# Drains on GpSimd, later row sums and fills, and no clearing of stored tiles in a fused FFT, expert and softplus kernel

## The chip, the cores and the metric

The kernel runs on one core of a Trainium2 chip. The time is that of one execution on the device, in microseconds (us), of the core that takes longest; here there is one. The engines are named as in the profile: PE (TensorE matmuls) and PEld (its weight loads), DVE (VectorE), ACT (ScalarE), POOL (GpSimd) and SP (SyncE, which here only issues DMAs). A q behind the name (POOLq) is the engine's sequencer: instructions that move no tensor data, such as waits, branches and drains.

## What is computed

Three stages follow each other. A real FFT filter over each of 8 batches of 3072 tokens with 256 channels; a top-1 mixture of 8 experts with room for `capacity` = 768 tokens each; and a softplus layer over all 24576 tokens.

```python
Y = np.fft.rfft(x, axis=1) * F;  y = np.fft.irfft(Y, n=S, axis=1)       # per batch
e = argmax(y @ w_gate);  slots 0..767 of each expert are filled in order of the tokens
y2 = gate_w * (relu(tok @ w1[e]) @ w2[e])          # tokens without a slot: zeros
h = y2 @ w_in;  g = np.maximum(h, 0.0) + np.log1p(np.exp(-np.abs(h)))
out = g @ w_out
```

For a token without a slot y2 is zero, so g is ln 2 everywhere and its row of the output is ln 2 times the sums of w_out's columns. All such rows are equal.

## The kernel before

The experts fill up early, so the kernel runs the filter and the gating for the first three batches only (STATIC = 3) and keeps a branch for the other case, which is not entered here (`tc.If` on `flag`, read by every engine at the end, L1266 and L1267).

The 8 × 768 slots are 16 units of 384 slots (class `Unit`). A unit gathers its tokens (`load_x`, three indirect DMAs of 128 rows issued by POOL, tile xd, L704), transposes them, multiplies by w1 and w2 (py, yh, yl), then runs 16 blocks of the softplus layer: `wi` makes pi in PSUM (L791), ACT takes abs, exp and ln (L649 to L652), DVE adds up g (L657), ACT rounds it to gh (L803), POOL makes the rest gl = g - gh (L808), and `wo` adds gh·woh, gh·wol and gl·woh into po (L823). At a unit's end `take` copies po to three tiles ot on DVE (L830), and `store` scatters them with three indirect DMAs that POOL issues (L835). POOL also splits the experts' weights (w1l and w2l, L689).

The order is written out by hand from step 16 on. A step t is one block of one unit, t = 16 v + i. `ev(t, order, ...)` files a call under its step, and `step(t)` runs a step's calls by their order W2, WI, SP, WO, SUM, W1, TAKE, TR, AHEAD. Block t has its `wi` and softplus in step t, its gh and gl in step t + 2 (`sp_split`), its `wo` in step t + 4. Each engine runs its instructions in the order in which they were written, so what stands first on an engine holds up what stands behind it. Three tiles g go around, so g of one block waits for gl of the block three before. There are seven tiles ot.

Class `Rest` makes the rows of tokens without a slot. `sums(k, c)` is one reduction on DVE over 32 columns of woh or wol (tile cs, L851), 16 of them; `zero` makes ln 2 (zt); `rows` multiplies (pz, L863) and copies the result to cs; `fill(a)` is one DMA of 512 KB from SP that writes that row over 512 tokens of the output (L869). The first 18 fills cover the three batches that have slots, and the stores of the units wait for them, since they write over the fills. The other 30 fills go out later at every third step and are declared free of the stores.

After the last step three memsets on POOL clear the first column of the last unit's tiles ot (L1259). A memset may start when the store that reads the tile has landed. Then come the flag's load (L1266), the branch (L1267) and the end of the program (L1407).

Of the kernel before, what the change touches and what calls it, by code (L numbers as in the profile page):

```python
# [17 lines left out]
NB, S, D, E = 8, 3072, 256, 8  # L18
# [8 lines left out]
STATIC = 3  # L27
# [174 lines left out]
def body(tc, cap, x, ff, fx, wg, w1, w2, win, wout, m1, m2, m3, m4, small, out):  # L202
    nc = tc.nc
# [671 lines left out]
    with tc.manual_schedule():  # L875
# [17 lines left out]
        units = [Unit(e, h) for h in range(nunit) for e in range(E)]  # L893
# [201 lines left out]
        W2, WI, SP, WO, SUM, W1, TAKE, TR, AHEAD = range(9)  # L1095
# [21 lines left out]
        for v in range(HEAD):  # L1117
            u = units[v]
# [53 lines left out]
        for v, u in enumerate(units):  # L1172
            for i in range(KI):
                t = 16 * v + i
# [33 lines left out]
        def ev(t, order, fn, *args):  # L1208
            if t < STEPS:
                return  # L1210
            at.setdefault(t, []).append((order, len(at.get(t, ())), fn, args))

        def step(t):
            for *_, fn, args in sorted(at.pop(t, ()), key=lambda e: e[:2]):
                fn(*args)
# [12 lines left out]
        rest = Rest()  # L1228
        for v, i in to_split:
            ev(split_at(v, i), AHEAD, split_w)  # L1230
        for v, u in enumerate(units):
            b = 16 * (v - 2)
            if v >= HEAD:
                ev(b - 16, AHEAD, load_x, u)
                for k in range(2):
                    ev(b - 7 + 2 * k, TR, u.tr_x, k)
            for j in range(8 if v > 1 else 0):
                ev(b + 2 * j - 3, W1, u.w1, j)
                ev(b + 2 * j, W2, u.w2, j)
            for i in range(KI):  # L1240
                t = 16 * v + i
                ev(t, WI, u.wi, i)
                ev(t + 2, SP - 0.5, u.sp_split, i)
                ev(t, SP, u.sp_act, i)
                ev(t, SUM, u.sp_sum, i)
                ev(t + 4, WO, u.wo, i)
            ev(16 * v + 19, TAKE, u.take)
            for t in range(3):
                ev(max(16 * v + 21, 40 + 3 * v) + t * (v < len(units) - 1), AHEAD, u.store, "out", [t])
        for t in range(16):  # L1250
            ev(16 + t // 2, SUM, rest.sums, t // 8, t % 8)
        ev(24, SUM, rest.zero)
        ev(26, TR, rest.rows)
        for a in range(NT // 512):
            ev(28 + a // 2 if a < STATIC * S // 512 else 3 * a, AHEAD, rest.fill, a)
        for t in range(min(at), max(at) + 1):
            step(t)
        for ot in units[-1].ot:
            nc.gpsimd.memset(ot[:, 0:1], 0.0)  # L1259
        stm.close()  # L1260
        stw.close()
        P.close.close()
# [4 lines left out]
    with tc.If(fv > 0):  # L1267
# [53 lines left out]
        with ExitStack() as st:  # L1321
# [9 lines left out]
            with tc.For_i(0, E, 1) as e:  # L1331
                with tc.For_i(0, nunit, 1) as h:
                    u = Unit(e, h)
# [77 lines left out]
```

## Time and profile before

| | |
|---|---|
| median of 3 runs | 1059.43 us (1055.43 to 1059.56) |
| the profiled execution | 1056.44 us |
| its span, first to last instruction | 1054.7 us |
| PE busy | 1024.0 us, 97% |
| ACT, POOL, DVE busy | 778.3, 598.9, 467.9 us |

The span says how long the program ran between its first and last instruction on the chip; the execution's own time has 1.7 us around it. A share of busy time is a mean over stages: the filter stage runs to about 205 us, the written-out steps from 290 us to about 1035 us, and the end of the program after that. Step t can be found in the trace by its six matmuls `pi` of L791: those of step 20 begin at 303.00 us, those of step 48 at 397.61 us, those of step 64 at 449.14 us.

### The profile page before, as it was taken

To read this page: it belongs to the slowest core of one execution; us is meant where nothing else is said; L and a number is where in the kernel's file an instruction comes from. 1 tells how busy PE (TensorE), PEld (TensorE's weight loads), DVE (VectorE), ACT (ScalarE), POOL (GpSimd) and SP (SyncE) were. 2 spreads that over 40 slices of the span, in tenths; PEclk is the share of its full clock that TensorE was granted. 3 is DMA by queue.
4 is the path that set the end of the run, shared out by engine and by line. 5 is a ranking of instruction groups with operands and counts; after the bars stand their busy time and mean duration, and the time that the engine had idled before them with its cause. 6 is when DMAs were issued, how large, how long until landed. Compare 5 with 4: busy or idle time off the path is not lost.

```text
span 1054.7 us, 19035 instructions
## 1 busy us (share of the span) xinstructions
PE 1024.0 (97%) x7112; PEld 952.2 (90%) x7112; DVE 467.9 (44%) x895; ACT 778.3 (74%) x1612; POOL 598.9 (57%) x563
## 2 busy tenths in 40 slices
PE   8999999999999999999999999999999999999992
PEld 7655676699999999999999999999999999999992
DVE  3855898888874332333232333233333333323220
ACT  4465478778867787777787878787877787878981
POOL 0512544688654676565757575757575756564552
PEclk9999999999999999999999999999999999999996
DMA  9977728654114822333323232322121211000000
GB/s 279 292 233 233 230 86 269 196 176 150 55 46 156 298 71 80 110 104 115 127 99 133 85 130 100 111 80 72 43 77 46 66 51 61 21 16 6 11 17 18
DMA packets 72823, 120.04 MB, mean 114 GB/s; under 512 B 6928, under 2 KB 46736, under 8 KB 72720
## 3 DMA queue, kind: packets, MB, share of 16 engines
q1 hardware_dynamic: 65424, 96.69, 28.9%
q0 software_dynamic: 4608, 12.59, 3.4%
q10 hardware_dynamic: 2688, 9.44, 2.7%
q8 instruction: 58, 0.95, 0.4%
q14 instruction: 45, 0.37, 0.1%
HBM read 71.51 MB, written 47.19 MB: 113 GB/s over the span
## 4 chain that ended last, share of the span: by engine, by line
PE 87%; DMA 4%; issue 2%; POOL 2%; DVE 2%; ACT 1%; SPq 0%; POOLq 0%; ACTq 0%; DVEq 0%
PE pi L791 24%; PE po L823 24%; PE pw L737 13%; PE py L766 12%; PE p L437 3%; PE p L385 2%; PE p L332 2%; PE p L398 2%; DMA xt<-in_x_dram 2%; DMA fr<-in_ff_dram 2%; PE p L357 1%; POOL gl L808 1%; PE pt L714 1%; PE p L536 1%; DMA fi<-in_fx_dram 1%
## 5 line engine op out<-in xcount | busy, mean ns | idle before, releaser
L657 DVE SCALAR_TENSOR_TENSOR g<-pi,ln 128x384 f32<-128x384 f32 x256 | 142.6, 557 | 490.2 <-ACT ln L652 450.0
L808 POOL TENSOR_TENSOR gl<-g,gh 128x384 fp32r<-128x384 f32 x256 | 260.8, 1022 | 112.2 <-ACT gh L803 106.1
L823 PE MATMUL po<-woh,gh 128*128 128x256 f32 x768 | 216.4, 282 | 3.9 <-DVE ot L830 3.9
L823 PE MATMUL po<-woh,gl 128*128 128x256 f32 x768 | 216.2, 281 | 0.0
L823 PE MATMUL po<-wol,gh 128*128 128x256 f32 x768 | 216.0, 281 | 0.0
L649 ACT ACTIVATE ab<-pi 128x384 f32<-128x384 f32 x256 | 124.7, 487 | 121.7 <-PE pi L791 98.3
L791 PE MATMUL pi<-yh,wih 128*128 128x384 f32 x512 | 172.8, 338 | 1.0 <-DVE g L657 1.0
L791 PE MATMUL pi<-yh,wil 128*128 128x384 f32 x512 | 173.1, 338 | 0.0
L791 PE MATMUL pi<-yl,wih 128*128 128x384 f32 x512 | 172.9, 338 | 0.0
L823 PEld LDWEIGHTS po<-woh,gh 128*128 128x128 f32 x768 | 144.0, 187 | 6.4 <-ACT ab L649 2.5
L823 PEld LDWEIGHTS po<-wol,gh 128*128 128x128 f32 x768 | 145.0, 189 | 0.0
L823 PEld LDWEIGHTS po<-woh,gl 128*128 128x128 f32 x768 | 144.7, 188 | 0.0
L652 ACT ACTIVATE ln<-ab 128x384 f32<-128x384 f32 (+1 forms) x257 | 134.8, 525 | 8.2
L650 ACT ACTIVATE ab<-ab 128x384 f32<-128x384 f32 (+1 forms) x257 | 134.7, 524 | 8.2
L689 POOL TENSOR_TENSOR w1l<-ws,w1h 128x512 fp32r<-128x512 f32 x64 | 83.2, 1301 | 100.1 <-ACT w1h L684 71.0
L803 ACT CAST gh<-g 128x384 fp32r<-128x384 f32 x256 | 130.2, 509 | 0.7 <-DVE g L657 0.5
L689 POOL TENSOR_TENSOR w2l<-ws,w2h 128x512 fp32r<-128x512 f32 x64 | 83.1, 1300 | 75.1 <-ACT w2h L684 73.9
L791 PEld LDWEIGHTS pi<-yh,wih 128*128 128x128 f32 x512 | 96.2, 188 | 1.3 <-DVE g L657 1.3
L791 PEld LDWEIGHTS pi<-yl,wih 128*128 128x128 f32 x512 | 96.2, 188 | 0.0
L791 PEld LDWEIGHTS pi<-yh,wil 128*128 128x128 f32 x512 | 96.2, 188 | 0.0
L377 POOL TENSOR_TENSOR z<-z,t 128x512 f32<-128x512 f32 x36 | 45.9, 1276 | 76.0 <-DVE t L372 60.9
L766 PE MATMUL py<-hh,w2h 128*128 128x384 f32 x256 | 88.2, 344 | 0.0
(141 smaller groups left out, 1897.4 us busy)
## 6 DMA issues: line engine op xcount, KB each, us to landing
ws<-in_w_dram SPq DMA_DIRECT2D x128, 256.0 KB
out_dram<-cs SPq DMA_DIRECT2D x48, 512.0 KB
xt<-in_x_dram SPq DMA_DIRECT2D x24, 384.0 KB
mid<-s ACTq DMA_DIRECT2D x16, 384.0 KB
rowsd<-yt SPq DMA_DIRECT2D x16, 384.0 KB
it<-mid SPq DMA_DIRECT2D x24, 256.0 KB
wst<-in_win_dram SPq DMA_DIRECT2D x8, 512.0 KB
wst<-in_wout_dram SPq DMA_DIRECT2D x8, 512.0 KB
```

The lines of the kernel that those rows point to most:

```text
L377: nc.gpsimd.tensor_tensor(out=z, in0=z, in1=t2, op=ALU.add)
L649: nc.scalar.activation(out=ab[:, :n], in_=h, func=ACTF.Abs)
L650: nc.scalar.activation(out=ab[:, :n], in_=ab[:, :n], func=ACTF.Exp, scale=-1.0)
L652: nc.scalar.activation(out=ln[:, :n], in_=ab[:, :n], func=ACTF.Ln, bias=1.0)
L657: nc.vector.scalar_tensor_tensor(out=g[:, :n], in0=h, scalar=0.0, in1=ln[:, :n], op0=ALU.max, op1=ALU.add)
L689: nc.gpsimd.tensor_tensor(out=lo, in0=self.ws.pop(i), in1=hi.bitcast(F32), op=ALU.subtract)
L737: nc.tensor.matmul(ps, lhsT=a[:, k, fs], rhs=b[:, k], start=(n == 0), stop=(n == 5))
L766: nc.tensor.matmul(self.py[d], lhsT=a[:, j % 2, ds], rhs=b, start=(j == 0 and n == 0), stop=(j == 7 and n == 2))
L791: nc.tensor.matmul(pi, lhsT=a[i // 2][:, i % 2, k], rhs=b[:, k], start=(n == 0), stop=(n == 5))
L803: nc.scalar.copy(gh, self.g[i])
L808: nc.gpsimd.tensor_tensor(out=gl, in0=g, in1=gh.bitcast(F32), op=ALU.subtract)
L823: nc.tensor.matmul(self.po[t], lhsT=a[:, ts], rhs=b[:, i], skip_group_check=True, start=(i == 0 and n == 0 and t != 1), stop=(i == KI - 1 ...
```

## The change

Four things change in the written-out steps.

- A `drain` on POOL is put at the end of step 16 v + 13 of each unit. Calls for steps below 16 are dropped, so there are 15 drains, in steps 29, 45, ..., 253. The program gives them no wait and no tensor.
- The 16 row sums stand one in a step in steps 16 to 31 (two in a step in steps 16 to 23 before), and at the step's end (AHEAD) where they stood behind g (SUM).
- The rows are made in step 33 (26 before), the 18 fills begin in step 35 (28 before), and the stores of the first two units begin in steps 46 and 49 (40 and 43 before). From the third unit on the stores stay where they were.
- The three memsets on the last unit's tiles ot are gone.

```diff
-                ev(max(16 * v + 21, 40 + 3 * v) + t * (v < len(units) - 1), AHEAD, u.store, "out", [t])
+                ev(max(16 * v + 21, 46 + 3 * v) + t * (v < len(units) - 1), AHEAD, u.store, "out", [t])
+            ev(16 * v + 13, AHEAD, nc.gpsimd.drain)
         for t in range(16):
-            ev(16 + t // 2, SUM, rest.sums, t // 8, t % 8)
+            ev(16 + t, AHEAD, rest.sums, t // 8, t % 8)
         ev(24, SUM, rest.zero)
-        ev(26, TR, rest.rows)
+        ev(33, TR, rest.rows)
         for a in range(NT // 512):
-            ev(28 + a // 2 if a < STATIC * S // 512 else 3 * a, AHEAD, rest.fill, a)
+            ev(35 + a // 2 if a < STATIC * S // 512 else 3 * a, AHEAD, rest.fill, a)
         for t in range(min(at), max(at) + 1):
             step(t)
-        for ot in units[-1].ot:
-            nc.gpsimd.memset(ot[:, 0:1], 0.0)
```

DVE's row at the end of the first unit, steps 18 to 20, before. A row is a line, an operation, out<-in and the size; cs is a row sum, hl a part of the expert layer, ot the copies that free po.

```order
L657 SCALAR_TENSOR_TENSOR g<-pi,ln 128x384
L851 TENSOR_REDUCE cs<-woh 128x32 x2
L657 SCALAR_TENSOR_TENSOR g<-pi,ln 128x384
L851 TENSOR_REDUCE cs<-woh 128x32 x2
L749 SCALAR_TENSOR_TENSOR hl<-pw,hh 128x384
L830 COPY ot<-po 128x256 x3
L657 SCALAR_TENSOR_TENSOR g<-pi,ln 128x384
```

The same place after the change.

```order
L657 SCALAR_TENSOR_TENSOR g<-pi,ln 128x384
L851 TENSOR_REDUCE cs<-woh 128x32
L657 SCALAR_TENSOR_TENSOR g<-pi,ln 128x384
L749 SCALAR_TENSOR_TENSOR hl<-pw,hh 128x384
L830 COPY ot<-po 128x256 x3
L851 TENSOR_REDUCE cs<-woh 128x32
L657 SCALAR_TENSOR_TENSOR g<-pi,ln 128x384
```

The two sums that stood ahead of hl and of the copies ot in step 19 are one sum behind them.

POOL's row in steps 48 to 51, before. w1l and w2l are weight splits, the DMA of xd is the gather for a later unit.

```order
L689 TENSOR_TENSOR w1l<-ws,w1h 128x512
L704 DMA xd<-rowsd,gi_2361 128x256 x3
L808 TENSOR_TENSOR gl<-g,gh 128x384 x2
L689 TENSOR_TENSOR w2l<-ws,w2h 128x512
L808 TENSOR_TENSOR gl<-g,gh 128x384 x2
```

The same place after the change, from the split in step 48 to gl in step 51 (the stores of steps 46 and 47 stand further up).

```order
L689 TENSOR_TENSOR w1l<-ws,w1h 128x512
L835 DMA out_dram<-ot,si_2362 24576x256
L704 DMA xd<-rowsd,gi_2361 128x256 x3
L808 TENSOR_TENSOR gl<-g,gh 128x384
L835 DMA out_dram<-ot,si_2362 24576x256
L808 TENSOR_TENSOR gl<-g,gh 128x384
L689 TENSOR_TENSOR w2l<-ws,w2h 128x512
L835 DMA out_dram<-ot,si_2362 24576x256
L808 TENSOR_TENSOR gl<-g,gh 128x384
```

The stores of the first two units, which stood in steps 40 to 45 with no gather near, now stand around the gather of step 48. The drains are not in these listings, which leave out instructions without tensors; a drain of step 16 v + 13 stands on POOL behind gl of that step and ahead of gl of the next.

## Rows read from the trace of the kernel before

**Rows 1.** The page, engines: busy us, share of the span, instructions.

```profile
PE 1024.0 (97%) x7112; PEld 952.2 (90%) x7112; DVE 467.9 (44%) x895; ACT 778.3 (74%) x1612; POOL 598.9 (57%) x563
```

**Rows 2.** Busy time by stretch: us; PE, PEld, DVE, ACT, POOL; clock; DMA share, GB/s.

```profile
290.00:340.00 50.00, 47.04 (x309) 46.26 (x309) 29.12 (x45) 36.08 (x78) 25.70 (x24) 1.00 0.26 84
340.00:957.00 617.00, 617.00 (x4096) 614.63 (x4095) 194.86 (x370) 478.98 (x1004) 386.02 (x357) 1.00 0.27 92
1035.00:1054.70 19.70, 0.78 (x7) 0.57 (x5) 1.09 (x3) 0.00 (x0) 3.27 (x6) 0.59 0.07 24
```

**Rows 3.** Timeline of PE, step 20: start, us, instruction [idle before <- releaser].

```profile
303.87 0.34 PE L791 MATMUL pi<-yh,wil 128*128 128x384 f32 x1
306.19 0.36 PE L823 MATMUL po<-woh,gh 128*128 128x256 f32 x1 [1.99 <-DVE ot L830]
```

**Rows 4.** Timeline of DVE, step 19.

```profile
302.93 1.99 DVE L851 TENSOR_REDUCE cs<-woh 128x32 f32<-128x512 f32 x2
304.84 0.55 DVE L749 SCALAR_TENSOR_TENSOR hl<-pw,hh 128x384 fp32r<-128x384 f32 x1
305.30 1.07 DVE L830 COPY ot<-po 128x256 f32<-128x256 f32 x3
```

**Rows 5.** Timeline of POOL, steps 48 to 50.

```profile
401.04 1.30 POOL L689 TENSOR_TENSOR w1l<-ws,w1h 128x512 fp32r<-128x512 f32 x1 [2.29 <-ACT w1h L684]
402.49 1.04 POOL L704 DMA_INDIRECT xd<-rowsd,gi  x1
...
406.17 2.01 POOL L808 TENSOR_TENSOR gl<-g,gh 128x384 fp32r<-128x384 f32 x2
```

**Rows 6.** Timeline of POOL, step 45: a store behind gl.

```profile
392.02 1.00 POOL L835 DMA_INDIRECT out_dram<-ot,si  x1 [0.17 <-issue]
```

**Rows 7.** Timeline of PE, step 51: the first matmul that reads gl.

```profile
407.37 0.29 PE L823 MATMUL po<-woh,gl 128*128 128x256 f32 x1
```

**Rows 8.** Busy time by stretch, around the end of the first fills.

```profile
360.00:363.00 3.00, 3.00 (x24) 3.00 (x24) 0.56 (x1) 2.90 (x7) 0.80 (x1) 1.00 1.02 380
366.00:370.00 4.00, 4.00 (x31) 4.00 (x30) 0.56 (x1) 3.46 (x8) 1.71 (x3) 1.00 0.00 0
```

**Rows 9.** Timeline of POOL, the last store and the memsets.

```profile
1038.75 0.98 POOL L835 DMA_INDIRECT out_dram<-ot,si  x1 [0.30 <-issue]
...
1041.93 0.10 POOL L1259 MEMSET ot<- 128x1 f32 x1 [1.93 <-DMA out_dram<-ot,si]
```

**Rows 10.** Lines L1266, L1267: engine, operation, count: ns min/median/max, first and last start.

```profile
L1266 POOLq TENSOR_LOAD <-flag x1: 502/502/502, 1041.9 to 1041.9; - x1
L1267 POOLq INC_SWDGE_SEM  x1: 2112/2112/2112, 1043.3 to 1043.3; - x1
```

**Rows 11.** Drains at the end (L1407) and the start (L1401) of the program.

```profile
L1407 POOLq DRAIN  x3: 40/107/8049, 1045.8 to 1054.4; - x3
L1407 ACTq DRAIN  x2: 8/8/8, 1036.0 to 1054.1; - x2
...
L1401 POOLq DRAIN  x1: 181/181/181, 0.3 to 0.3; - x1
```

**Rows 12.** The page, DMA issues: POOL's indirect DMAs.

```profile
xd<-rowsd,gi POOLq DMA_INDIRECT x48
out_dram<-ot,si POOLq DMA_INDIRECT x48
```

**Rows 13.** Timeline of POOL, steps 61 to 64, around the place of the third drain.

```profile
443.96 1.02 POOL L808 TENSOR_TENSOR gl<-g,gh 128x384 fp32r<-128x384 f32 x1 [1.80 <-ACT gh L803]
446.23 1.30 POOL L689 TENSOR_TENSOR w2l<-ws,w2h 128x512 fp32r<-128x512 f32 x1 [1.25 <-ACT w2h L684]
...
449.27 1.01 POOL L808 TENSOR_TENSOR gl<-g,gh 128x384 fp32r<-128x384 f32 x1 [0.76 <-ACT gh L803]
452.58 1.30 POOL L689 TENSOR_TENSOR w1l<-ws,w1h 128x512 fp32r<-128x512 f32 x1 [2.29 <-ACT w1h L684]
```

**Rows 14.** Timeline of PE, step 64: the first matmul that reads gl of step 62.

```profile
450.42 0.28 PE L823 MATMUL po<-woh,gl 128*128 128x256 f32 x1
```

## The prediction

> **What bounds the kernel now.** I read the page's line of engines first: PE is busy 97% of the span [rows 1]. That leaves the question where the other 3% lie, so I cut the written-out steps into stretches [rows 2]. From 340 to 957 us PE is busy all of 617.00 us: in these steps nothing can be won, and an edit there can only cost. Two stretches have room. From 290 to 340 us PE lacks 2.96 us. From 1035 us on it has 0.78 us of work in 19.70 us: PE, ACT and DVE are done, and POOL runs alone to the end. The largest piece of that end is one row: of the three drains on POOL in the program's last lines one takes 8.049 us, starting at 1045.8 us [rows 11]. It ends at 1053.8 us, 0.9 us before the span does. So the change has to be judged at four places: the stall at 304 us, the memsets, the long drain, and whatever the added instructions delay in steps where PE has no slack.
>
> **The row sums.** In step 20 the last matmul of `wi` starts at 303.87 us and the next one, the first of `wo`, at 306.19 us, with 1.99 us of idle time that the copies ot ended [rows 3]. DVE shows why: two sums of 1.99 us in all, then hl, then ot from 305.30 us [rows 4]. In the new order the sums of that step stand behind ot. Without the 1.99 us ahead of them hl and ot would start about 1.9 us earlier, limited by when hl's input is there, and later units, which have no sums at all, show no such stall: PE is full there [rows 2]. I take 2.0 us as won; the bounds are 1.0 us (if the single sum of step 18 still pushes) and 2.0 us. The sums that move to steps 24 to 31 lie on DVE, which is busy 194.86 of 617 us from 340 us on [rows 2]; at one sum of about 1.0 us [rows 4] in a step of about 3.2 us they fit behind g. I cost them at nothing; if one delayed a copy ot or a g, it would be by at most its own 1.0 us, once or twice. Rows and fills are the same instructions in later steps and PE pays for them as before.
>
> **The stores that meet the gather.** This is a cost. Before, in step 48, POOL has w1l at 401.04 us, the three gathers from 402.49 us, and gl of step 49 at 406.17 us [rows 5]; as two gl take 2.01 us it ends at 407.18 us. PE reads that gl at 407.37 us without a wait [rows 7]: 0.2 us to spare. Now the stores of steps 46 to 51 stand there, and the one of step 48 is ahead of the gathers. A store costs 1.00 us and 0.17 us of issue behind gl, or 0.30 us behind another indirect DMA [rows 6, 9]. So gl of step 49 comes 1.3 us later, at 408.5 us, and PE waits 1.1 to 1.2 us at step 51. Behind it POOL has a store, gl of step 50, a split, a store and gl of step 51: 1.1 + 1.0 + 1.3 + 1.1 + 1.0 us, which ends at 414.0 us. The reader of that last gl stands two steps of 3.2 us behind the one of 407.37 us, and PE is 1.2 us late: 415.0 us, in time. I take +1.2 us, bounds 0 and +2. The fills are over before these stores: the DMA engines are full to 363 us and at zero from 366 us [rows 8], so the 18 fills end near 365 us for a first store in step 40; both move by seven and six steps, and the margin of some 11 us shrinks by one step of 3.2 us. Nothing waits there.
>
> **The memsets.** The last store is issued at 1038.75 us, and the third memset starts at 1041.93 us, after 1.93 us of waiting for its landing [rows 9]. The flag's load follows at once [rows 10]. Without the memsets it can follow the store's end at 1039.73 us. That is 2.2 us earlier for everything behind it on POOL. What is late next is SP, which waits at the end for the same store; that lands before 1041.93 us, while POOL would still be in its 2.112 us semaphore instruction [rows 10], from about 1041.1 to 1043.2 us. So the whole 2.2 us should show; the lower bound is 0, if that instruction or the drain behind it itself waits for the store.
>
> **The drains.** What a drain on POOL costs in mid-kernel no row shows, so it is bounded. Below: 0.04 us and 0.107 us at the end, where the long drain stands just ahead, and 0.181 us at the start [rows 11]. Above: 8.049 us. What sets the long one apart is what went before it on POOL without a drain: all 563 of its instructions [rows 1], among them 96 indirect DMAs [rows 12]. ACT's drains take 8 ns after 1612 instructions [rows 11, 1], so it is not their number in general; it is something that POOL alone leaves behind, and the indirect DMAs are what POOL alone issues. I take the time as growing with these since the last drain: 8.049/96 = 0.084 us each. Then an added drain, with 3 to 15 of them behind it, takes 0.25 to 1.3 us. POOL has room for that: around step 61 it idles 1.80, 1.25, 0.76 and 2.29 us [rows 13], together 6.1 us before the split of step 64. Cost 0. After the last added drain, in step 253, only the last unit's three stores come, so the final drain would take 0.25 us and its floor, say 0.3 us. It gives 7.75 us; the bounds are 0 and 8.0 us.
>
> The Trainium skill speaks against this: "VectorE: DVE Perf Modes", section "The DRAIN you can't avoid", says that the drains which a program's start and end bring along take a constant 12 ns or so on all five engines. By that rule no edit could shorten the final one. The trace agrees for ACT (8 ns) and not for POOL (8.049 us), so I follow the trace, but the idea behind the rule, a length that this program doesn't set, is the second rival below.
>
> **The sum.** Against the profiled execution of 1056.44 us: -2.0 (sums) + 1.2 (stores) - 2.2 (memsets) - 7.75 (drain) = -10.75 us, which is 1045.7 us. The three timed runs have a median of 1059.43 us, 3.0 us above that execution; from the median the same sum gives 1048.7 us. I name 1047 us, between the two.
>
> **Rivals.** First, the forecast: the drain's length follows the indirect DMAs since the last drain. For it: the row at the start and the two short rows at the end had none since the previous drain. Against it: one long row is one point, and a straight line through it is my choice.
>
> Second, the final drain keeps its length, for a reason that the added ones don't touch (the branch's end, the store just issued, the 2.112 us semaphore instruction ahead of it), and the added ones are short, as their last indirect DMA is six steps back. Then only the rest counts: -2.0 + 1.2 - 2.2 = -3.0 us, 1053.4 us by the profiled execution and 1056.4 us by the median. For it: the long drain comes right behind the last stores. If the end also waits for a set time after the last store, the memsets give nothing either and it is -1 us.
>
> Third, slower: any drain on POOL after an indirect DMA takes the full 8.05 us, whatever their number. The place decides. Behind gl of step 61, which ends at 443.96 - 1.80 = 442.16 us [rows 13], such a drain lasts to 450.2 us; gl of step 62 then ends at 451.2 us instead of 444.98 us, and PE, which reads it at 450.42 us [rows 14], waits 0.8 us. The split of step 64 comes some 2 us late, and so does the gl behind the next gathers, which is just in time now [rows 5, 7]: 1 us more where a gather follows (11 of 15 drains). That is 11 × 1.8 + 4 × 0.8 = 23 us, and the final drain keeps its 8 us: 1056.4 - 3.0 + 23 = 1076 us. It decides from a drain of about 6.1 us on, POOL's idle time there; shorter ones are hidden. Against it: the short drains show that a drain as such is cheap.
>
> **How the numbers follow.** Forecast 0.60, second rival 0.25, third 0.12, and 0.03 for the rest, such as a stall at the stores or sums larger than I price it. For the forecast's own ends: the sums may give 1 us less, the stores 0.8 us more, and the 2.112 us instruction ahead of the drain [rows 10] could shrink with what the drains take off POOL, by up to 2 us. That reaches from 1043.5 to about 1050 us over both bases. To hold 8 in 10 the range must take in the second rival to 1056.5 us: 1043.5 to 1056.5 us. A measurement of this kernel can tell about 0.5% or 5.3 us from no change. The forecast is faster by 1.0%; the second rival is within it (0.3%); the third is slower by 1.9%. Chances: faster 0.61, same 0.26, slower 0.13.
>
> **What would show it.** In the profile after: the wait of po for ot near 304 us gone; a new wait of about 1.2 us of a matmul po for gl in step 51, near 405 us; POOL's flag load right behind the last store; 15 drains in the steps, each under 1.5 us, those behind twelve or fifteen indirect DMAs longer than those behind three; the last drain well under 1 us; PE otherwise full from 340 to 950 us. If the last drain still takes about 8 us and the others are short, the second rival holds; if the others take 8 us and PE waits for gl in each unit's last steps, the third.

## The result, and the profile after

The changed kernel takes 1044.22 us (median of 4 runs, 1043.35 to 1046.03) beside 1058.44 us for the kernel before on the same chip (4 runs): a ratio of 0.9872, 95% interval 0.9846 to 0.9899. That is faster, inside the range of 1043.5 to 1056.5 us, 0.7 us above its lower end and 2.8 us below the 1047 us named. The span of the profiled execution falls from 1054.7 to 1041.9 us.

The page's line of engines and the busy time by stretch (us; PE, PEld, DVE, ACT, POOL; clock; DMA share, GB/s), of the changed kernel:

```profile
PE 1023.2 (98%) x7112; PEld 951.2 (91%) x7112; DVE 468.1 (45%) x895; ACT 777.7 (75%) x1612; POOL 597.1 (57%) x560
```

```profile
290.00:340.00 50.00, 49.03 (x328) 48.51 (x327) 29.95 (x46) 38.86 (x83) 26.62 (x25) 1.00 0.15 46
340.00:957.00 617.00, 615.99 (x4086) 613.32 (x4085) 195.11 (x370) 477.43 (x1001) 384.33 (x357) 1.00 0.28 95
```

Not all of the difference between the medians is the change's. In its profiled execution the kernel before spent 3.41 us of the filter stage at a granted clock of 0.50, the lower of TensorE's two levels (1.2 GHz). PE had been busy for 8.17 of the 10 us ahead of it, and for the same 8.17 us in the changed kernel, whose clock stayed at 1.00. First before, then after:

```profile
199.00:202.41 3.41, 3.41 (x13) 2.77 (x13) 2.41 (x5) 1.33 (x3) 2.95 (x3) 0.50 0.83 272
199.00:202.41 3.41, 3.02 (x18) 2.53 (x17) 2.80 (x6) 1.48 (x4) 2.96 (x3) 1.00 0.78 278
```

Over all later runs of the kernel before, those with a mean granted clock of 0.993 took 1055.2 to 1056.0 us, and those with 0.988 or 0.989 took 1059.3 to 1060.0 us. The fastest runs of the two kernels, 1055.43 and 1043.35 us, are 12.1 us apart, and the rows below account for 12.0 us.

Against [rows 2], PE wins 1.99 us in the first stretch and loses 1.01 us in the second. The losses have names in PE's waits from 285 us on (engine, line, waited for: us in total, times, longest):

```profile
PE po L823 <- DVE ot L830: 1.9, 2, 1.0
PE po L823 <- POOL gl L808: 1.0, 1, 1.0
PE pi L791 <- DVE g L657: 1.0, 1, 1.0
```

The kernel before has the first at 3.9 us in three times and the second not at all; the third, in step 26, it has too. In PE's timeline the stall of [rows 3] is gone: `wi` ends and `wo` begins without idle time.

```profile
303.10 0.34 PE L791 MATMUL pi<-yh,wil 128*128 128x384 f32 x1
303.28 0.36 PE L823 MATMUL po<-woh,gh 128*128 128x256 f32 x1
```

The new wait stands in step 51, where [rows 7] had none:

```profile
404.34 0.28 PE L823 MATMUL po<-wol,gh 128*128 128x256 f32 x1
405.63 0.39 PE L823 MATMUL po<-woh,gl 128*128 128x256 f32 x1 [1.01 <-POOL gl L808]
```

POOL's timeline shows what gl stood behind, the store ahead of the three gathers (compare [rows 5]):

```profile
398.14 1.30 POOL L689 TENSOR_TENSOR w1l<-ws,w1h 128x512 fp32r<-128x512 f32 x1 [0.57 <-ACT w1h L684]
399.59 1.00 POOL L835 DMA_INDIRECT out_dram<-ot,si  x1
400.89 1.04 POOL L704 DMA_INDIRECT xd<-rowsd,gi  x1 [0.30 <-issue]
...
404.56 1.01 POOL L808 TENSOR_TENSOR gl<-g,gh 128x384 fp32r<-128x384 f32 x1
```

Most of the gain is behind the last step. The last store in POOL's timeline, then the rows of the program's end (line, engine, operation, count: ns min/median/max, first and last start), and the added drains:

```profile
1037.18 0.98 POOL L835 DMA_INDIRECT out_dram<-ot,si  x1 [0.30 <-issue]
```

```profile
L1265 POOLq TENSOR_LOAD <-flag x1: 504/504/504, 1035.6 to 1035.6; - x1
L1266 POOLq COMPARE_BRANCH  x1: 58/58/58, 1036.1 to 1036.1; - x1
L1266 POOLq INC_SWDGE_SEM  x1: 236/236/236, 1039.0 to 1039.0; - x1
L1406 POOLq DRAIN  x3: 46/107/1288, 1039.3 to 1041.6; - x3
```

```profile
L1215 POOLq DRAIN  x15: 1361/2454/3222, 333.4 to 1024.5; - x15
```

From the last store's end to the span's end the kernel before took 1054.7 - 1039.73 = 14.97 us [rows 9]; now it is 1041.9 - 1038.16 = 3.74 us, 11.2 us less. Three rows changed against [rows 10, 11]: the long drain from 8.049 to 1.288 us, the semaphore instruction from 2.112 to 0.236 us, and the flag's load, which ran at 1035.6 us, ahead of the second and third store. What the long drain now waits for is the landing of the last store. That store lands 3.2 us after its start, at 1037.18 + 3.2 = 1040.4 us, and the drain ends at 1039.3 + 1.29 = 1040.6 us:

```profile
DMA to landing us min/median/max: 3.2/3.2/3.2
```

In the five executions that have added drains ahead of the last stores, no memsets, and this landing in their trace, the long drain ends 0.15 to 0.16 us behind it.

The record of an added drain begins while the gl ahead of it still runs, so its 1.4 to 3.2 us are not its price. The first ends at 333.4 + 3.2 = 336.6 us, 1.3 us behind that gl, which ends at 335.33 us:

```profile
334.31 1.02 POOL L808 TENSOR_TENSOR gl<-g,gh 128x384 fp32r<-128x384 f32 x1
337.13 1.02 POOL L808 TENSOR_TENSOR gl<-g,gh 128x384 fp32r<-128x384 f32 x1 [1.80 <-ACT gh L803]
```

The next gl waits for ACT and not for the drain. Read the same way, the drains behind three indirect DMAs take 0.32 us, behind six 0.56 us, behind twelve 1.05 us.

### The profile page after: what moved, and what is told of

The parts are those of the page before. It is cut to its first block, busy times and chain, and to the rows that moved or that the text cites. A ratio compares the mean times of both kernels' runs of the same rounds, so it can differ in the third digit from the quotient of the medians.

```text
span 1041.9 us, 19044 instructions
## 1 busy us (share of the span) xinstructions
PE 1023.2 (98%) x7112; PEld 951.2 (91%) x7112; DVE 468.1 (45%) x895; ACT 777.7 (75%) x1612; POOL 597.1 (57%) x560
## 4 chain that ended last, share of the span: by engine, by line
PE 90%; POOL 2%; DMA 2%; issue 2%; DVE 2%; ACT 1%; POOLq 0%; ACTq 0%; DVEq 0%; SPq 0%
PE pi L791 24%; PE po L823 24%; PE pw L737 13%; PE py L766 12%; PE p L437 3%; PE p L385 2%; PE p L332 2%; PE p L398 2%; PE p L309 1%; PE p L357 1%; POOL gl L808 1%; DMA xt<-in_x_dram 1%; PE pt L714 1%; PE p L536 1%; DMA fi<-in_fx_dram 1%
```

## Experiments

The theory is the forecast: a drain's length follows the indirect DMAs issued on POOL since the last one, and PE sees none of the added drains. The rivals are a final drain of fixed length and drains that each take 8 us.

**One part at a time.** The kernel before with the 15 drains added:

```diff
                 ev(max(16 * v + 21, 40 + 3 * v) + t * (v < len(units) - 1), AHEAD, u.store, "out", [t])
+            ev(16 * v + 13, AHEAD, nc.gpsimd.drain)
```

> The kernel before with the 15 drains alone; sums, fills, stores and memsets as before. Theory (count): a drain takes 0.08 us plus 0.083 us for each indirect DMA on POOL since the last drain, after the work ahead of it has ended. The final drain, with 3 of them behind it and all landed, then takes 0.33 us instead of 8.05 us; if the semaphore instruction ahead of it (2.11 us before, 0.24 us after the change) follows the same count, it takes 0.24 us: 9.6 us less in all. If that instruction was shortened by the missing memsets instead, it keeps 2.1 us and the kernel gains 7.7 us. Rival (the end sets the final drain, the memsets' removal is what shortened it): final drain 8 us, no gain.

Measured: 1049.24 us (ratio 0.9917, 0.9894 to 0.994; the kernel before 1057.61 us beside it). The final drain, with three stores since the last one:

```profile
L1408 POOLq DRAIN  x3: 46/107/289, 1045.3 to 1046.6; - x3
```

From the last store's end to the span's end it is 7.4 us, so 7.5 us of the 14.97 are gone by the drains alone. Both rivals fall: the drain shortens, and PE's waits are those of the kernel before. That holds although one of the added drains, in step 45, stands behind a store that is still in flight and takes 5.5 us:

```profile
L1215 POOLq DRAIN  x15: 1361/2461/5498, 336.8 to 1025.8; - x15
```

But the final drain (-7.76 us) and the semaphore instruction (2.112 to 0.236 us) together shortened by 9.6 us, 2.1 us more than the end did. The rows of the branch tell where that went, first before, then here:

```profile
L1267 POOLq COMPARE_BRANCH  x1: 45/45/45, 1042.5 to 1042.5; - x1
L1267 POOLq EVENT_SEMAPHORE  x4: 17/30/43, 1043.0 to 1043.2; - x4
```

```profile
L1268 POOLq COMPARE_BRANCH  x1: 58/58/58, 1042.1 to 1042.1; - x1
L1268 POOLq EVENT_SEMAPHORE  x4: 17/30/43, 1044.7 to 1044.9; - x4
L1268 POOLq INC_SWDGE_SEM  x1: 236/236/236, 1045.0 to 1045.0; - x1
```

The first instruction behind the branch comes 0.5 us after it in one kernel and 2.6 us after it in the other. What the semaphore instruction won, this gap took, and so the end is 7.5 us shorter and not the 9.6 us expected. The DMA queues show what moved meanwhile. In the gap, from 1042.2 to 1044.6 us, it is one packet alone, of the kind instruction; in the kernel before one such packet moves too, between 1043.3 and 1045.4 us, beside the semaphore instruction of 2.112 us. First here, then before (queue, kind: packets, MB, share of 16 engines):

```profile
q14 instruction: 1, 0.01, 1.0%
q14 instruction: 1, 0.01, 1.6%
```

So POOL's instructions may have been late here, but no experiment shows that the gap waits for this packet.

The memsets alone removed:

```diff
-        for ot in units[-1].ot:
-            nc.gpsimd.memset(ot[:, 0:1], 0.0)
```

> The kernel before without the three memsets, nothing else changed. Theory (count): the final drain has 96 indirect DMAs behind it and keeps 8.05 us, the semaphore instruction keeps 2.1 us; the end comes 2.2 to 2.7 us earlier, as POOL no longer waits for the last store. Rival (the missing memsets shortened the end): final drain 1.3 us or semaphore instruction 0.24 us, 4 to 11 us less.

Measured: 1052.99 us (ratio 0.9945, 0.9928 to 0.9962). The end got 4.4 us shorter, twice the term of the sum. The 4.6 us between the medians lie in the rival's range, but its cause is absent: the final drain and the semaphore instruction keep their lengths. The last store, and the end's rows:

```profile
1038.82 0.99 POOL L835 DMA_INDIRECT out_dram<-ot,si  x1 [0.31 <-issue]
```

```profile
L1264 POOLq TENSOR_LOAD <-flag x1: 499/499/499, 1037.2 to 1037.2; - x1
L1265 POOLq INC_SWDGE_SEM  x1: 2096/2096/2096, 1039.1 to 1039.1; - x1
L1405 POOLq DRAIN  x3: 40/107/7905, 1041.3 to 1050.0; - x3
```

The load starts 1.6 us ahead of the last store's start, and the semaphore instruction runs beside that store. The memsets had held up the load, the branch and this instruction as well as costing their own wait. The long drain stays at 7.9 us, so it isn't the memsets that made it long.

The moved sums, fills and stores alone (the changed kernel without drains, with the memsets):

```diff
-            ev(16 * v + 13, AHEAD, nc.gpsimd.drain)
...
         for t in range(min(at), max(at) + 1):
             step(t)
+        for ot in units[-1].ot:
+            nc.gpsimd.memset(ot[:, 0:1], 0.0)
```

> Sums, rows, fills and stores moved as in the change; no drains, memsets kept. Theory: the wait of po for ot in step 20 (2.0 us) is gone, a wait of po for gl of about 1.0 us in step 51 is new: the last store is issued about 0.9 us earlier, less or more what the filter stage varies by itself. The final drain keeps 8.05 us. Rival (the moved work has a part in the short end): the end after the last store shorter than 14.9 us.

Measured: 1056.71 us, ratio 0.999 (0.9978 to 1.0001), 0.9 us by the medians, which the interval doesn't tell from no change. The trace decides: PE's waits for ot fall to 2.0 us, the wait for gl of 1.0 us is there without any drain, and the steps from 16 to 255 take 0.93 us less. The drain takes 7.905 us and the end after the last store 14.9 us, so the moved work has no part in the short end. By the medians the three parts alone give -8.4, -4.6 and -0.9 us, -13.9 us together, and the whole change -14.2 us. By the traces they don't quite add up: the end falls by 7.5 us for the drains and by 4.4 us for the memsets, and by 11.2 us, not 11.9 us, for both.

**What sets a drain's length.** Four drains instead of fifteen, on the kernel before:

```diff
+            if v % 4 == 3:
+                ev(16 * v + 13, AHEAD, nc.gpsimd.drain)
```

> The kernel before with a drain only in steps 61, 125, 189 and 253, behind 30, 24, 24 and 15 indirect DMAs. Theory (count): 2.6, 2.1, 2.1 and 1.3 us past the end of the gl ahead of each, and 0.33 us for the final drain, with PE full in the steps; as fast as with 15 drains. Rival (a drain costs what the instructions since the last one cost, whatever they are: 96 to 99 tensor instructions here against 24): four times the 0.3 to 1.3 us that 15 drains took.

Measured: 1050.6 us (one run). That is 1.4 us above the fifteen drains, but not by the drains: step 21, where none stands, ran 1.5 us longer than in the kernel before, at a granted clock of 0.76 in the mean from 307 to 314 us (about half of it at the lower level, 1.2 GHz), behind PE's 1.9 us of idle time in step 20. A single drain, in step 189:

```diff
+            if v == 11:
+                ev(16 * v + 13, AHEAD, nc.gpsimd.drain)
```

> The kernel before with one drain, in step 189, behind 78 indirect DMAs. Theory (count): 0.08 + 78 x 0.083 = 6.6 us past the end of the gl ahead of it; 18 are left for the final drain, 1.6 us. By the third rival's price a drain of over 6.1 us begins to cost: the gl behind it is still in time, the one behind the gathers of step 192 is late, so PE waits up to 1 us between steps 192 and 196. Rival (a length that doesn't depend on the count): 1 to 2 us for this drain, as the 15 took, and no wait of PE.

Measured: 1051.22 us (one run). The added drains and the final ones of both, then POOL's timeline around the single drain:

```profile
L1215 POOLq DRAIN  x4: 2342/3929/4430, 442.2 to 1027.9; - x4
L1409 POOLq DRAIN  x3: 52/107/294, 1047.3 to 1048.5; - x3
```

```profile
L1215 POOLq DRAIN  x1: 8353/8353/8353, 853.5 to 853.5; - x1
L1409 POOLq DRAIN  x3: 52/107/1529, 1047.1 to 1049.2; - x3
L1269 POOLq INC_SWDGE_SEM  x1: 536/536/536, 1046.5 to 1046.5; - x1
```

```profile
854.39 1.03 POOL L808 TENSOR_TENSOR gl<-g,gh 128x384 fp32r<-128x384 f32 x1
862.03 1.02 POOL L808 TENSOR_TENSOR gl<-g,gh 128x384 fp32r<-128x384 f32 x1 [6.61 <-PE pw L737]
```

The single drain ends at 853.5 + 8.35 = 861.85 us, 6.4 us behind the gl ahead of it, with 78 indirect DMAs since the start; the final one has 18 and takes 1.53 us. The releaser that the row names is not what held gl up: POOL stood in the drain. Together:

| indirect DMAs since the last drain | drain, us | where |
|---|---|---|
| 0 | 0.05 | final, behind a drain that follows the last store (further down) |
| 3 | 0.29 | final, drains alone and every fourth |
| 15 | 1.3 | first added, changed kernel |
| 18 | 1.53 | final, one drain |
| 24 and 30 | 2.03 and 2.5 | every fourth, past the gl ahead |
| 78 | 6.4 | one drain, past the gl ahead |
| 96 | 7.9 to 8.05 | final, the kernels without added drains |

From 18 to 78 that is (6.4 - 1.53) / 60 = 0.081 us for each, from 3 to 18 (1.53 - 0.29) / 15 = 0.083 us. The gl and splits in between don't count: behind three gathers and 24 of them a drain takes 0.32 us, behind three stores and 16 of them 0.31 us. Every indirect DMA of this kernel moves 128 rows, so no run here tells their number from the number of rows. The list of PE's waits has no new one in either kernel. But the single drain does cost a little, in the place that the expectation named: gl behind the gathers of step 192 starts at 871.34 us, the first matmul that reads it starts 0.39 us behind the matmul ahead of it, where 0.12 us is usual, and step 195 takes 0.37 us longer than in the kernel before.

```profile
872.04 0.28 PE L823 MATMUL po<-wol,gh 128*128 128x256 f32 x1
872.43 0.39 PE L823 MATMUL po<-woh,gl 128*128 128x256 f32 x1
```

So 6.4 us is just past what POOL's idle time covers there; the prediction's estimate for that limit was 6.1 us.

**Where the drain stands.** The changed kernel with its drains in step 16 v + 23, which from the third unit on is right behind the unit's third store. A sixteenth drain comes in by it, in step 263 behind the program's last stores:

```diff
-            ev(16 * v + 13, AHEAD, nc.gpsimd.drain)
+            ev(16 * v + 23, AHEAD, nc.gpsimd.drain)
```

> The changed kernel with its drains moved to step 16 v + 23, right behind the third store of a unit. Theory (count, and waits for what is in flight): the count is again 6 for most units, 0.56 us, but the drain ends no earlier than the store lands, about 2.1 us after the store's own end: drains of over 2 us past the store's end, hidden in the steps. At the end of the program the drain behind the last store holds the flag's load back until the store has landed, which gives back about 2 us. Rival (a drain doesn't wait for DMAs in flight): 0.56 us past the store's end.

Measured: 1049.4 us (one run), 5.2 us above the changed kernel's median. The span is 5.7 us longer: 3.7 us at the end, and 2.1 us ahead of step 16, where none of these drains stands. The drains' records are 2.75 us longer at the median, and PE's waits are the changed kernel's:

```profile
L1215 POOLq DRAIN  x16: 2224/5204/5475, 314.6 to 1037.6; - x16
```

```profile
1015.10 1.00 POOL L835 DMA_INDIRECT out_dram<-ot,si  x1 [0.17 <-issue]
1017.83 1.99 POOL L808 TENSOR_TENSOR gl<-g,gh 128x384 fp32r<-128x384 f32 x2 [1.73 <-ACT ln L652]
```

```profile
DMA to landing us min/median/max: 2.4/2.4/2.4
```

The first fence is the added drains, the second a store and the gl behind its drain, the third the time from that store's start to its landing. The store lands at 1015.10 + 2.4 = 1017.5 us and POOL goes on at 1017.8 us: the drain waits until the store has landed. The last one, behind the last stores, held up the flag's load to 1042.4 us, so nothing could run ahead; that is the 7.4 us from the last store's end to the span's end, against 3.7 us: the end gives back 3.7 us, where about 2 us were expected. The program's own drain has no indirect DMA behind it any more and is the 53 ns of this row:

```profile
L1406 POOLq DRAIN  x3: 46/53/107, 1046.1 to 1047.3; - x3
```

**The wait that the stores brought.** The theory was that any store beside the gather of step 48 makes gl late. The stores of the first two units in steps 45 to 47 and 50 to 52:

```diff
-                ev(max(16 * v + 21, 46 + 3 * v) + t * (v < len(units) - 1), AHEAD, u.store, "out", [t])
+                ev({0: 45, 1: 50}.get(v, 16 * v + 21) + t * (v < len(units) - 1), AHEAD, u.store, "out", [t])
```

> The changed kernel with the stores of the first unit in steps 45 to 47 and of the second in steps 50 to 52, so that no store stands in step 48 ahead of the gathers. Theory: the wait of po for gl in step 51 (1.0 us of idle time) is gone and nothing takes its place; 1.2 us earlier at the last store, too little for the times to tell, so the trace decides. Rival (the wait comes from the backlog of all six stores): a wait of 0.5 us or more in steps 51 to 55.

The same, with ln 2 (zt) made in step 31 (`ev(31, SUM, rest.zero)`) instead of 24:

> As the kernel with the stores apart, and the constant of ln 2 (zt) made in step 31 instead of 24, where no transposes for the next unit stand in the step behind it. Theory: the wait of pi for g in step 26 (1.0 us of idle time) goes too, as ACT's 1.85 us for zt then fall where PE has a PSUM tile to spare; 1.1 us less than with the stores apart, 2.3 us less than the changed kernel: about 1042 us. Rival: the wait moves along to step 32 or 33.

Measured: 1044.34 us (1042.91 to 1044.99) and 1043.53 us (1042.98 to 1044.13); the wait of pi for g in step 26 went with zt, but po still waits 0.8 us for gl in step 51 in both. That expectation missed, and the sign of its rival, a wait of 0.5 us or more, is there. POOL's timeline with the stores apart shows why:

```profile
388.89 1.03 POOL L835 DMA_INDIRECT out_dram<-ot,si  x1
393.54 1.01 POOL L808 TENSOR_TENSOR gl<-g,gh 128x384 fp32r<-128x384 f32 x1 [3.62 <-ACT ab L649]
...
400.20 1.30 POOL L689 TENSOR_TENSOR w1l<-ws,w1h 128x512 fp32r<-128x512 f32 x1
...
405.34 1.98 POOL L808 TENSOR_TENSOR gl<-g,gh 128x384 fp32r<-128x384 f32 x2
```

The drain of step 45 now stands behind the first of these stores and waits for its landing: POOL lies still for 3.62 us, two more stores follow, and the split in step 48, which waits 0.57 us for its input in the changed kernel, is late itself. With the drains alone, where a drain stood behind a store in this step too but no store followed, POOL caught up. So the second theory: the stores would be free there if no drain stood behind them. Two kernels tell them apart, one with the stores apart, ln 2 in step 31 and no drain in step 45, the other the changed kernel without that drain alone:

```diff
-            ev(16 * v + 13, AHEAD, nc.gpsimd.drain)
+            if v != 2:
+                ev(16 * v + 13, AHEAD, nc.gpsimd.drain)
```

> The stores apart from the gather (steps 45 to 47 and 50 to 52), ln 2 in step 31, and the drain of step 45 left out; the drain of step 61 then answers for more indirect DMAs. Theory (the wait that stayed in step 51 came from the drain of step 45, which stood behind a store still in flight and kept POOL about 3.5 us past the work ahead of it): the split w1l in step 48 waits for ACT again instead of being late, gl of step 50 begins some 2 us earlier than with that drain, PE's wait for gl in step 51 is gone, and the span falls by about 0.9 us to some 1041.1 us. Rival (the gather of step 48 and the two splits alone fill POOL's time before gl): the idle time of 0.8 us in step 51 stays, and the span too. Both: the end is the changed kernel's, the last drain between 1.0 and 1.4 us.

> The changed kernel without the drain of step 45 alone. Theory (there the drain stands ahead of all stores, is short and hidden, and the wait in step 51 comes from the stores of steps 46 to 49 around the gather): the idle time of 1.0 us before po in step 51 stays, the span is 1041.9 us within run-to-run differences of the filter stage. Rival (any drain ahead of that gather makes POOL late): the wait goes, and the span falls by about 1 us.

Measured: 1042.18 us (1040.94 to 1042.76, 5 runs; ratio 0.9844, 0.983 to 0.9857) and 1046.25 us (one run). In the first, the split waits for ACT again and gl starts 2.2 us earlier:

```profile
398.00 1.30 POOL L689 TENSOR_TENSOR w1l<-ws,w1h 128x512 fp32r<-128x512 f32 x1 [0.59 <-ACT w1h L684]
...
403.14 2.00 POOL L808 TENSOR_TENSOR gl<-g,gh 128x384 fp32r<-128x384 f32 x2
```

PE's waits from 290 us on are then a single row, the first that the changed kernel has, and PE is busy 50.00 of 50 us and 617.00 of 617 us in the two stretches. In the second kernel the wait in step 51 is the changed kernel's:

```profile
407.82 0.39 PE L823 MATMUL po<-woh,gl 128*128 128x256 f32 x1 [1.01 <-POOL gl L808]
```

It starts 2.2 us later than in the changed kernel, because this execution's filter stage took that much longer; its drain had been short and hidden. So the wait in the changed kernel is the stores', as it was with the moved parts alone; with the stores apart it took the drain and the stores behind it. Last, the changed kernel and the version without waits on the same chip:

> The changed kernel, beside the next one on the same chip. Both theories: about 1044.2 us, as it had.

> The kernel with the stores apart, ln 2 in step 31 and no drain in step 45, again, beside the changed kernel. Theory (its two waits of PE, 1.17 us for gl in step 51 and about 1 us for ln 2 in step 26, were on the path to the end, and their absence is not taken back by anything): about 2.0 us less than the changed kernel. Rival (the difference of 2.0 us between the calls was the filter stage's own from run to run): the same time within 0.7 us.

Measured: 1045.12 us (1043.49 to 1045.74) and 1042.64 us (1042.34 to 1043.77), 2.5 us apart; their intervals against the kernel before, 0.986 to 0.9896 and 0.9845 to 0.9878, still overlap. The traces tell that it isn't the filter stage: the steps from 16 to 255 take 2.6 us less, 1.28 us of it in step 51 and 1.27 us in steps 25 and 26. The version without waits has the lowest median of all the kernels, both times.

## Why the prediction held, and where it didn't

- **The bound.** That only the two stretches had room was right: PE won 1.99 us in the first, and the end gave 11.2 us.
- **The row sums.** 2.0 us named. The idle time of 1.99 us is gone and step 20, from its first `pi` to the next step's, takes 2.19 us for 4.33 us, 2.14 us less. The sums moved to steps 24 to 31 brought no new wait, and the rows cost in step 33 (0.86 us) what steps 26 and 27 won (0.82 us).
- **The stores.** 1.2 us named; PE idles 1.01 us and step 51 takes 1.27 us longer. The mechanism was the one worked out, and in the trace of the moved parts alone the steps win 0.93 us, for the 0.8 us that both terms make.
- **The memsets.** 2.2 us named, 4.4 us measured alone, and 7.4 - 3.7 = 3.7 us on top of the drains. The step that failed is "without the memsets it can follow the store's end". The load ran ahead of stores that were still queued, and so did the branch, so the load stands ahead of the last store and not right behind it, as the prediction's signs had it. The order of writing, by which an engine's first instruction holds up the next, does not hold between POOL's queued stores and these instructions of its sequencer. What remains behind the store is the drain, which waits for its landing.
- **The drains.** The law was right, 0.084 us by one point and 0.082 us by the table, and so was the cover: none of the 15 shows on PE. The final drain's size was wrong: 1.29 us for "well under 1 us". Behind the same three stores it takes 0.29 us once they have landed, as with the memsets in place. Without the memsets, which waited for the landing, the drain waits for it. So 6.76 us came from this row, not 7.75. That the drains alone shortened the end by 7.5 us, close to the 7.75 us named, is partly luck: the drain and the semaphore instruction together gave 9.6 us, and the gap behind the branch took 2.1 us back.
- **The semaphore instruction.** Its shrinking was left to the range, "by up to 2 us". It shrank by 1.88 us. In the drains alone the gap behind the branch took this back; in the changed kernel that gap (1036.1 to 1038.7 us) lies beside the stores.
- **The sum.** From the first `pi` of step 16 to that of step 255 the changed kernel takes 0.78 us less, and the end 11.2 us: -12.0 us for the -10.75 us named. The span fell by 12.8 us; the other 0.80 us is what the stages before step 16 were shorter in this execution (the first `pi` of step 16 starts at 289.54 us and started at 290.34 us). The change touches nothing there, and the lower clock shown above, which only the execution before had, lies in these stages. Of the 2.8 us between the median and the number named, 1.3 us is the step from the sum's 1045.7 us to 1047 us, halfway to the other base; in the sum itself the memset term was 1.5 us too small, and the semaphore instruction had none, while the final drain's was 1.0 us too large.
- **The page's rule.** The Trainium skill, "VectorE: DVE Perf Modes", section "The DRAIN you can't avoid", has a constant 12 ns or so on all engines for a program's end. On POOL the runs give 0.29 to 8.05 us for the same drain by what the program issued; here the measurement decides.

## What to carry to other kernels

Where the last row of a profile is a long drain on POOL, count the indirect DMAs since the last one: a drain in a step where POOL idles pays for them early, beside other work. Put it ahead of the unit's stores and not behind one that is still in flight, and make sure that its own length fits the idle time there (here 5.5 us were hidden, and 6.4 us cost PE 0.37 us). Look at whatever waits for a landing just ahead of the program's end, since it also holds up instructions that would otherwise have run beside the last transfers.

## What the runs showed of the hardware

- A drain on POOL took about 0.05 us and 0.082 us for each indirect DMA of 128 rows since the last drain (0 to 96 of them), and it also waited for those in flight to land (1.29 us for 0.29 us at the end, ending 0.16 us behind the landing). The two run beside each other: behind 96 it took 7.905 us with the last store in flight (memsets removed) and with all landed (moved parts alone).
- The semaphore instruction behind the branch goes the same way, 0.171 us with none (drains behind the stores), 0.236 us with 3, 0.536 us with 18 and 2.1 us with 96: 0.02 us for each.
- POOL's load of the flag and its branch ran while two and one of the three stores written ahead of them were still to start (1035.6 and 1036.1 us; stores at 1035.9 and 1037.2 us).
- Behind the branch, the next instruction on POOL came after 0.5 us in the kernels without added drains and after some 2.6 us in those with 14 to 16 (in some of them beside the last stores). With one drain a pause of 2 us stands a few instructions further, ahead of the semaphore instruction (1044.5 to 1046.5 us), with four it stands among the four instructions ahead of that (1044.6 to 1046.7 us). So its place goes with the number of instructions ahead, as far as these kernels show. In each of these pauses a packet of instructions moves, and with the drains alone (one, four or fifteen added to the kernel before) it is the only packet of any kind. That fits a wait for instructions, but no experiment shows it, and the cause stays open.
